# Top-32 attention and a SoLU layer on one core: steps of two chunks from each of two head pairs, with the weight check at the end

## The chip, the core and the metric

The kernel runs on one core of one Trainium2 chip. The core has a tensor engine (PE), a vector engine (DVE), a scalar engine (ACT), a general engine (POOL) and DMA queues that SyncE (SP) issues. Each engine works through its own instructions in order; across engines they wait for each other by semaphores. The metric is the time of one execution in device microseconds, smaller is better: a median over runs, beside one further execution that was profiled.

## The reference

```python
scores = scale * np.matmul(q, k.transpose(0, 1, 3, 2))          # B=8, H=8, S=576, D=64
kth = np.partition(scores, -32, axis=-1)[..., -32:-31]
scores = np.where(scores >= kth, scores, -1e9)
attn = softmax(scores)                                           # only the 32 largest of a row
x = (attn @ v).transpose(0, 2, 1, 3).reshape(4608, 512)
h = x @ w_in                                                     # 512 -> 1024
solu = h * softmax(h)
ln = (solu - mean(solu)) / sqrt(var(solu) + 1e-6) * g_ln
out = ln @ w_out                                                 # 1024 -> 512
```

The weights arrive as 64-bit numbers, everything is computed in 32 bits.

## The kernel before

The work is in `fast_path`. A general path behind it runs only if a flag (`bad`) is set at the end; it isn't reached here.

**A step** is one pair of heads of one batch (32 steps). Its 576 queries are four chunks of 128 and a tail of 64; with two heads that gives eight tiles of 128 queries x 576 keys, and a ninth in which the tails of both heads share the partitions. Per tile, the rank search and the softmax go through these instructions:

- PE forms scores (L816), ACT brings them to memory as `X` (L825).
- Counting. DVE counts the entries over a first threshold (`count0`, L833, tile `junkv`); two small operations form a second threshold (L841, L843). ACT counts against it (`count1`, a Sign with a sum, L849, tile `junka`). When all nine tiles are counted, `third` (L858, L862, L866 on DVE) forms the third threshold, and ACT counts again and leaves the signs (`count2`, L879, tile `sg`).
- Nearest. `side` (L888) picks a direction for three tiles at a time; `nearest` writes `w` on DVE (L900) and at once takes its eight largest (MAX8, L905). `kth` (five small DVE operations, L926 to L934) makes the exact 32nd largest value of all nine tiles.
- Softmax. ACT takes exponentials `E` (L913); DVE zeroes what lies under the 32nd and sums the rest (`keep`, L942); `inverse` (L950, L953) and POOL's `norm` (L957) divide.
- Product. PE transposes `E` (`tp_p` L971, `tp_pt` L1004), ACT copies to `PT` (L983 to L1012), PE multiplies with v (`om`, L1023), ACT copies to the token tiles `xTm` and `xTt` (L1034, L1037).

Ahead of a step its q, k and v are loaded and transposed, and PE and DVE estimate mean and spread of every row's scores (`y_ps` L737, `yq` L755, `ss` L766).

**A token tile** is 128 tokens of the second part; there are 36. PE `mm1` (`h_ps`, L1045), ACT `hexp` (L1056), DVE `solu` (L1061, L1064, L1068), ACT `square` (L1074), POOL `ln` (L1080 to L1085), PE transposes (`tp_ln`, L1092), ACT copies (L1098), PE `mm2` (`o_ps`, L1103), ACT copies to `osb` (L1110) and SP stores. A token tile needs all four head pairs of its queries, so the four tiles of batch b are placed beside steps 4(b+1) to 4(b+1)+3. The tails of two batches make one more tile. Those of the last batch come after the last step.

**Weights**: 16 pieces of 128x512. `w_bits` (three DVE operations, L579, L583, L587), `w_low` (ACT, L595), `w_mul`, `w_add` and `w_gain` (POOL) make 32-bit numbers; `w_check` (three ACT operations, L601, L604, L605) tests their exponents beside that.

**The order** is a table of places: every function has a number for a step, the step's index times 39 is added, and everything is sorted by that sum. The sorted order is the order in which PE, ACT, DVE and POOL get their instructions. DMA issues are not held to it. At the very end DVE counts in how many places the estimates and the weights lay in their bounds (`hit`, L1282), PE adds over partitions (`tp_ok`, L1287), and DVE sets `bad` (L1290), which the engines read and branch on.

Of the kernel before, what the change touches and what calls it, by code (L numbers as in the profile page):

```python
# [15 lines left out]
P = 128  # L16
# [427 lines left out]
def fast_path(  # L444
# [21 lines left out]

    nc = tc.nc
# [11 lines left out]
    SP = S // 2  # L479
# [69 lines left out]
    if not w_wide:  # L549
        nc.gpsimd.memset(w_ok, 512.0)  # L550
# [76 lines left out]
    st = [dict() for _ in pairs]  # L627
# [6 lines left out]
    def load_qk(i):  # L634
        b, hp = pairs[i]
        hh = slice(2 * hp, 2 * hp + 2)
        d = st[i]

        d["q"] = p1.tile([P, NT, D], F32, tag="qm", name="qm")
        d["k"] = p1.tile([P, 2 * NM, D], F32, tag="km", name="km")  # L640
        for nm, src in (("q", q), ("k", k)):
            nc.sync.dma_start(
                out=d[nm][:, 0 : 2 * NM, :].rearrange("p (t h) d -> p t h d", h=2),
                in_=src[b, hh, 0:SM, :].rearrange("h (p t) d -> p t h d", t=NM),
            )
# [26 lines left out]
    def pre_of(i):

        return once(st[i], "pre", lambda: ps_o.tile([P, 512], F32, tag="o", name="pre"))

    def prep_t(i):

        d = st[i]
        pre = pre_of(i)
        for n, nm in enumerate("qk"):  # L680
            nc.tensor.transpose(
                pre[:, n * ST : (n + 1) * ST], d[nm + "t"].rearrange("p h d -> p (h d)"),
# [3 lines left out]
    def prep_tc(i):  # L686
# [650 lines left out]
```

## Time and profile before

| | us |
|---|---|
| median of 3 runs (lowest to highest) | 1352.69 (1352.49 to 1354.34) |
| the profiled execution, its own time | 1354.09 |
| its span in the trace | 1352.3 |
| outside the span | 1.8 |
| PE, DVE, ACT, POOL busy, share of the span | 91%, 87%, 87%, 36% |
| chain of waits that ended last, by engine | DVE 52%, PE 27%, ACT 12% |

Busy time is an average over three different stretches. The page's strips cut the span into 40 slices of 33.8 us and give the busy share of each in tenths. In the first seven, when there are no token tiles or few, PE stands between 4 and 8 and its granted clock, at 9 in the first two, is at 6 or 7 tenths in the next four. From the ninth to the 36th PE stands at 9 with a clock at 9 (9 is 90% or more), and DVE and ACT at 8 or 9. In the last three PE works nearly alone: DVE stands at 0 or 1 and ACT at 2.

### The profile page before, as it was taken

How to read it: one execution, taken by the hardware profiler on the slowest of the kernel's cores; microseconds unless marked ns; L12 is line 12 of the kernel's file. 1: busy time of each engine (PE TensorE's matmuls, PEld its weight loads, DVE VectorE, ACT ScalarE, POOL GpSimd, SP SyncE). 2: the span in 40 equal slices, each digit the busy share in tenths (PEclk: the TensorE clock that was granted, in tenths of full speed). 3: DMA queues.
4: the chain of work that ended last, by engine and by line, in shares of the span. 5: the costliest groups of instructions: out<-in, count | busy, mean ns of one | idle time of the engine just before them, and what ended most of it. 6: DMA issues, size and time to landing. Idle time of an engine off the chain costs nothing.

```text
span 1352.3 us, 20269 instructions
## 1 busy us (share of the span) xinstructions
PE 1231.0 (91%) x6243; PEld 672.3 (50%) x6243; DVE 1183.2 (87%) x2766; ACT 1174.3 (87%) x2702; POOL 486.7 (36%) x584
## 2 busy tenths in 40 slices
PE   6476668999999999999999999999999999998997
PEld 3243434555555545555555545555555555554443
DVE  5799999999999989999999989899999989899010
ACT  6999899999999989899999989899999989896222
POOL 3245435443333323333333323333333333234110
PEclk9976679899999999999999999999999999999999
DMA  5112121011111111111111111111111111000001
GB/s 142 50 41 59 45 58 50 20 34 28 36 36 36 28 30 33 35 35 36 30 34 36 36 28 27 44 35 29 34 31 32 36 28 36 26 17 9 16 8 34
DMA packets 102404, 48.59 MB, mean 36 GB/s; under 512 B 87432, under 2 KB 95632, under 8 KB 102288
## 3 DMA queue, kind: packets, MB, share of 16 engines
q1 hardware_dynamic: 102288, 47.21, 13.0%
q8 instruction: 52, 0.85, 0.3%
q14 instruction: 64, 0.52, 0.1%
HBM read 37.75 MB, written 9.44 MB: 35 GB/s over the span
## 4 chain that ended last, share of the span: by engine, by line
DVE 52%; PE 27%; ACT 12%; issue 6%; DVEq 0%; ACTq 0%
DVE w L900 11%; DVE w L905 10%; DVE E L942 10%; PE o_ps L1103 8%; PE h_ps L1045 8%; DVE junkv L833 8%; ACT junka L849 4%; PE om L1023 3%; PE s_ps L816 3%; DVE solu L1064 2%; PE tp_p L971 2%; ACT sg L879 2%; DVE al L888 1%; ACT PT L983 1%; ACT X L825 1%
## 5 line engine op out<-in xcount | busy, mean ns | idle before, releaser
L957 POOL TENSOR_SCALAR E<-E,rden 128x576 f32<-128x576 f32 x256 | 239.3, 945 | 602.9 <-DVE step L858 496.6
L816 PE MATMUL s_ps<-qkT 64*128 64x288 f32 (+1 forms) x1280 | 259.1, 467 | 22.5 <-ACT X L825 11.6
L1103 PE MATMUL o_ps<-w_out,lnT 128*128 128x512 f32 x576 | 258.0, 593 | 0.0
L1045 PE MATMUL h_ps<-w_in,xTm 128*128 128x512 f32 x512 | 234.8, 603 | 0.0
L905 DVE MAX8 w<-w 128x8 f32<-128x576 f32 x288 | 219.2, 761 | 9.9
L900 DVE SCALAR_TENSOR_TENSOR w<-X,al,sg 128x576 f32<-128x576 f32 x256 | 220.9, 863 | 1.1
L942 DVE SCALAR_TENSOR_TENSOR E<-X,kth,E 128x576 f32<-128x576 f32 x256 | 212.2, 875 | 4.1 <-ACT junka L849 0.9
L879 ACT ACTIVATE sg<-X,t 128x576 bf16<-128x576 f32 x256 | 199.2, 787 | 15.5 <-DVE t L866 15.5
L849 ACT ACTIVATE junka<-X,t 128x576 bf16<-128x576 f32 x256 | 199.2, 801 | 2.1 <-DVE t L843 0.6
L816 PEld LDWEIGHTS s_ps<-qkT 64*128 64x128 f32 (+1 forms) x1280 | 143.1, 192 | 106.6 <-ACT X L825 38.4
L833 DVE TENSOR_SCALAR_CACHE_REDUCE junkv<-X,t 128x576 bf16<-128x576 f32 x256 | 192.0, 803 | 2.5 <-ACT X L825 2.5
L825 ACT ACTIVATE X<-s_ps 128x576 f32<-128x576 f32 x256 | 160.0, 660 | 34.5 <-PE s_ps L816 33.1
L971 PE MATMUL tp_p<-ident,E 128*128 128x128 f32 x1024 | 159.9, 293 | 13.2 <-POOL E L957 5.6
L1103 PEld LDWEIGHTS o_ps<-w_out,lnT 128*128 128x128 f32 x576 | 106.9, 190 | 120.9 <-issue 118.2
L913 ACT ACTIVATE E<-X 128x1152 f32<-128x1152 f32 x128 | 153.6, 1250 | 0.1
L983 ACT COPY PT<-tp_p 128x512 f32<-128x512 f32 x256 | 143.3, 606 | 7.8 <-PE tp_p L971 7.7
L971 PEld LDWEIGHTS tp_p<-ident,E 128*128 128x128 f32 x1024 | 117.0, 147 | 64.2 <-issue 20.2
L1045 PEld LDWEIGHTS h_ps<-w_in,xTm 128*128 128x128 f32 x512 | 92.7, 190 | 107.5 <-issue 106.0
L1023 PE MATMUL om<-PT,vm 128*64 128x288 f32 x1024 | 140.9, 418 | 0.0
L1023 PEld LDWEIGHTS om<-PT,vm 128*64 128x64 f32 x1024 | 68.9, 139 | 59.4 <-issue 20.6
L1056 ACT ACTIVATE e_sb<-h_ps 128x1024 f32<-128x1024 f32 x36 | 38.2, 1062 | 41.3 <-PE h_ps L1045 41.3
L1061 DVE RECIPROCAL rs<-sum_all 128x1 f32<-128x1 f32 x36 | 5.6, 156 | 64.7 <-ACT e_sb L1056 64.4
(132 smaller groups left out, 1706.4 us busy)
## 6 DMA issues: line engine op xcount, KB each, us to landing
qm<-in_q_dram SPq DMA_DIRECT2D x32, 256.0 KB, 3.4
km<-in_k_dram SPq DMA_DIRECT2D x32, 256.0 KB, 3.2
vm<-in_v_dram SPq DMA_DIRECT2D x32, 256.0 KB, 2.8
out_dram<-osb SPq DMA_DIRECT2D x32, 256.0 KB, 2.2
w_raw<-in_moe_w_in_dram SPq DMA_DIRECT2D x8, 512.0 KB, 3.8
w_raw<-in_moe_w_out_dram SPq DMA_DIRECT2D x8, 512.0 KB, 3.3
qt<-in_q_dram SPq DMA_DIRECT2D x32, 32.0 KB, 2.2
kt<-in_k_dram SPq DMA_DIRECT2D x32, 32.0 KB, 2.2
```

The lines of the kernel that those rows point to most:

```text
L816: nc.tensor.matmul(out=s[:, half, 0:SH], lhsT=qkT[hd, qs], rhs=qkT[hd, k0 : k0 + SH], start=True, stop=True,)
L833: nc.vector.tensor_scalar(out=junk, in0=x_of(i, j), scalar1=d["t0"][:, j : j + 1], scalar2=None, op0=ALU.is_ge, op1=ALU.add, accum_out=col ...
L849: nc.scalar.activation(out=junk, in_=x_of(i, j), func=AF.Sign, scale=-1.0, bias=d["t1"][:, j : j + 1], accum_out=columns(i, "n1")[:, j : j ...
L879: nc.scalar.activation(out=d["sg", j], in_=x_of(i, j), func=AF.Sign, scale=-(1.0 + 2.0**-23), bias=d["t2"][:, j : j + 1], accum_out=column ...
L900: nc.vector.scalar_tensor_tensor(out=w, in0=x_of(i, j), scalar=d["al"][:, j : j + 1], in1=d.pop(("sg", j)), op0=ALU.subtract, op1=ALU.mult,)
L905: nc.vector.max(w8[:, j, :], w)
L942: nc.vector.scalar_tensor_tensor(out=e, in0=x_of(i, j), scalar=d["kth"][:, j : j + 1], in1=e, op0=ALU.is_ge, op1=ALU.mult, accum_out=den_a ...
L957: nc.gpsimd.tensor_scalar(out=e, in0=e, scalar1=st[i]["rden"][:, j : j + 1], scalar2=1.0, op0=ALU.mult, op1=ALU.mult,)
L971: nc.tensor.transpose(tp[:, c, :], e[:, c * P : (c + 1) * P], ident)
L1023: nc.tensor.matmul(out=o[h * D : (h + 1) * D, 0:SP], lhsT=vm[:, h, c, :] if c < NM else vt[hd, :], rhs=pt[:, h * NM + c, :] if c < NM else ...
L1045: nc.tensor.matmul(out=h[:, half, :], lhsT=x[:, c, :], rhs=w_in[:, c, half * 512 : (half + 1) * 512], start=(c == 0), stop=(c == NP - 1),)
L1103: nc.tensor.matmul(out=o, lhsT=d["lnT"][:, c, :], rhs=w_out[:, c, :], start=(c == 0), stop=(c == NF - 1),)
```

## The change

- **Steps.** A step is now two chunks of one head pair and two chunks of another, of the same half of the batch, and the tail of one pair. Four steps still make a batch, and tiles, instructions on PE and their sizes stay as they were, except that the two attention products of a step are 320 and 256 columns wide and not 288 each. The work on k (`load_k`, `prep_k`, `moments`) is a list of its own, for each pair once. Both steps of a half need the keys of all four pairs. After two steps the first two token tiles of a batch are ready: they are placed beside step 4b+2+t, not 4(b+1)+t. After the last step three token tiles are left (two and the tails), not five.
- **Counts.** Of the nine `count1` of a step two (the second head of the fourth chunk, and the tails) go to DVE (L875). They count in another unit than ACT's, so `third` does its first two operations once for seven tiles and once for two.
- **MAX8 apart.** `nearest` is split in `nearest` (L953) and `best` (MAX8, L960), each with a place of its own.
- **Weight check.** `w_check` with its three ACT operations is gone from the start. Near the end all 16 pieces are loaded again into `X` buffers (`w_again`), DVE shifts out exponent bits (`w_exp`, L615), and one ACT operation each (L622) sums over them.
- **Buffers and copies.** `junkv`, `junka` and `osb` have one buffer, not two; k, v and the moments have four. One `copy_pt` instead of two, two instructions in `copy_last` instead of three, one copy of tails in `copy_v` instead of two per step.
- **Places.** All numbers of the table are new. q is loaded by four DMAs and not by one.

```diff
-    NPAIR = len(pairs)
+    steps = []
+    for b in range(B):
+        for half in range(2):
+            for n in range(NP // 2):
+                two = (2 * n + half, 2 * n + 1 - half)
+                chunks = [(hp, 2 * half + t) for hp in two for t in range(2)]
+                steps.append((b, chunks, two[0]))
+    NSTEP = len(steps)
...
+    def w_again(n):
+        raw = w_raw["again", n] = p8.tile([P, 512], mybir.dt.uint64, tag="X", name="w_again")
+        nc.sync.dma_start(out=raw, in_=w_chunks[n][1])
+
+    def w_exp(n):
+        w_tmp["exp", n] = p2.tile([P, 512], U32, tag="w", name="w_exp")
+        nc.vector.tensor_scalar(
+            out=w_tmp["exp", n], in0=words(("again", n), 1), scalar1=27, scalar2=15,
+            op0=ALU.logical_shift_right, op1=ALU.bitwise_and,
+        )
+
     def w_check(n):
-        f = low_of(n)[:, 1, :]
+        junk = p1.tile([P, S], BF16, tag="junka", name="junka")
         nc.scalar.activation(
-            out=f, in_=words(n, 1).bitcast(I32), func=AF.Square, scale=2.0**-27
-        )
-        nc.scalar.activation(out=f, in_=f, func=AF.Square, bias=m65)
-        nc.scalar.activation(
-            out=f, in_=f, func=AF.Sign, scale=-1.0, bias=p251, accum_out=w_ok[:, n : n + 1]
+            out=junk[:, 0:512], in_=w_tmp["exp", n].bitcast(I32), func=AF.Square, bias=m75,
+            accum_out=w_ok[:, n : n + 1],
         )
...
     def count1(i, j):
-        d = st[i]
-        junk = p2.tile([P, S], BF16, tag="junka", name="junka")
+        if j >= NT - N1:
+            count_v(i, j, "t1", "n1")
+            return
+        d = st[i]
+        junk = p1.tile([P, S], BF16, tag="junka", name="junka")
...
+        groups = ((slice(0, NT - N1), -513.0, -0.25), (slice(NT - N1, NT), -31.5, 0.5))
+        for js, less, _ in groups:
+            nc.vector.scalar_tensor_tensor(
+                out=w[:, js], in0=d["n1"][:, js], scalar=less, in1=d["tb"][:, js],
+                op0=ALU.add, op1=ALU.mult,
+            )
+        for js, _, part in groups:
+            nc.vector.scalar_tensor_tensor(
+                out=t2[:, js], in0=w[:, js], scalar=part, in1=d["t1"][:, js],
+                op0=ALU.mult, op1=ALU.add,
+            )
...
-        w = p2.tile([P, S], F32, tag="w", name="w")
+        w = d["w", j] = p2.tile([P, S], F32, tag="w", name="w")
...
+    def best(i, j):
         w8 = columns(i, "w8", NT * 8).rearrange("p (t e) -> p t e", e=8)
-        nc.vector.max(w8[:, j, :], w)
+        nc.vector.max(w8[:, j, :], st[i].pop(("w", j)))
...
-        (nearest, range(9), [41.97, 43.52, 51.69, 33.2, 29.56, 35.41, 57.15, 56.61, 53.25]),
+        (nearest, range(9), [41.07, 47.51, 39.3, 32.69, 29.76, 32.16, 57.74, 55.76, 51.21]),
+        (best, range(9), [46.43, 52.3, 45.06, 36.45, 31.16, 33.82, 59.19, 58.14, 52.97]),
...
-        n = NP * (b + 1)
-        last = b == B - 1
+        n = NP * b + 2
         for t in range(NM):
...
-            if last:
-                all_times(n * STEP + 15.0 * t, last_times, d)
+            if n + t >= NSTEP:
+                all_times(NSTEP * STEP + 15.0 * (n + t - NSTEP), last_times, d)
             else:
-                all_times((n + t) * STEP, token_times, d)
+                all_times((n + t) * STEP, token_times if b else first_times[t], d)
```

How the rows of the table now fall is seen in the instructions' order. First DVE within a step, at the nearest values: before, `w` (L900) and the MAX8 that reads it (L905) stand together, with the small operations of `inverse` (L950, L953) and `side` (L888) between the couples.

```order
L888 SCALAR_TENSOR_TENSOR al<-n_5442,tt 128x3
L900 SCALAR_TENSOR_TENSOR w<-X,al,sg 128x576
L905 MAX w_5568<-w 128x8
L950 TENSOR_SCALAR rden<-den_all 128x3
L953 RECIPROCAL rden<-rden 128x3
L900 SCALAR_TENSOR_TENSOR w<-X,al,sg 128x576
L905 MAX w_5568<-w 128x8
L888 SCALAR_TENSOR_TENSOR al<-n_5442,tt 128x3
L900 SCALAR_TENSOR_TENSOR w<-X,al,sg 128x576
L905 MAX w_5568<-w 128x8
L785 TENSOR_TENSOR t_5621<-mean,zs 128x9
L787 SCALAR_TENSOR_TENSOR ta<-tb,t_5621 128x9
```

After, on the same engine in a step: `w` is L953, MAX L960, and L875 are counts (into `c` against the first threshold, into `n` against the second); L941 is `side`, L886 and L888 are the two operations of the second threshold, L981 begins `kth`.

```order
L953 SCALAR_TENSOR_TENSOR w<-X,al,sg 128x576
L875 TENSOR_SCALAR junkv,c_4074<-Xt,t_4063 128x576
L941 SCALAR_TENSOR_TENSOR al<-n_3914,tt 128x3
L886 TENSOR_TENSOR u<-c_4074,tb 128x9
L888 TENSOR_TENSOR t_4194<-u,ta 128x9
L953 SCALAR_TENSOR_TENSOR w<-Xt,al,sg 128x576
L960 MAX w_4002<-w 128x8 x2
L953 SCALAR_TENSOR_TENSOR w<-X,al,sg 128x576
L875 TENSOR_SCALAR junkv,n_4220<-X,t_4194 128x576
L953 SCALAR_TENSOR_TENSOR w<-X,al,sg 128x576
L960 MAX w_4002<-w 128x8 x2
L981 TENSOR_TENSOR hot<-ranks,far 128x72
```

Something else now stands between a `w` and its own MAX, and the operation on the first counts (L886) no longer follows the last count directly.

DVE again, from the end of `kth` (L934 before) to `third` (L858 to L866), with the `keep`s (L942) around it; before:

```order
L931 TENSOR_REDUCE zk_all<-hot 128x9
L933 TENSOR_TENSOR kth<-al,zk_all 128x9
L934 SCALAR_TENSOR_TENSOR kth<-kth 128x9
L942 SCALAR_TENSOR_TENSOR E,den_all<-X,kth,E 128x576 x4
L950 TENSOR_SCALAR rden<-den_all 128x3
L953 RECIPROCAL rden<-rden 128x3
L858 SCALAR_TENSOR_TENSOR step<-n_5323,tb 128x9
L862 SCALAR_TENSOR_TENSOR t_5419<-step,t_5286 128x9
L866 TENSOR_SCALAR t_5419<-t_5419 128x9
L942 SCALAR_TENSOR_TENSOR E,den_all<-X,kth,E 128x576 x3
```

After, `kth` ends with L989, the `keep`s are L997, `third` is L909 to L919, and L875 is a count:

```order
L988 TENSOR_TENSOR kth<-al,zk_all 128x9
L989 SCALAR_TENSOR_TENSOR kth<-kth 128x9
L875 TENSOR_SCALAR junkv,n_4220<-Xt,t_4194 128x576
L997 SCALAR_TENSOR_TENSOR E,den_all<-X,kth,E 128x576 x3
L909 SCALAR_TENSOR_TENSOR step<-n_4220,tb 128x7
L909 SCALAR_TENSOR_TENSOR step<-n_4220,tb 128x2
L914 SCALAR_TENSOR_TENSOR t_4305<-step,t_4194 128x7
L914 SCALAR_TENSOR_TENSOR t_4305<-step,t_4194 128x2
L919 TENSOR_SCALAR t_4305<-t_4305 128x9
L997 SCALAR_TENSOR_TENSOR E,den_all<-X,kth,E 128x576 x3
```

A count stands between `kth` and the first `keep`, and `third` has five instructions in place of three.

PE after the last attention product, before (from the fourth row; ahead of it are 4 of `h_ps` and 8 of `o_ps`; a matmul of 512 columns counts once here, and twice in the trace):

```order
L1045 MATMUL h_ps<-w_in,xTm 128x512 x16
L1092 MATMUL tp_ln<-ident,solu 128x128 x8
L1045 MATMUL h_ps<-w_in,xTm 128x512 x4
L1103 MATMUL o_ps<-w_out,lnT 128x512 x4
L1045 MATMUL h_ps<-w_in,xTm 128x512 x4
L1092 MATMUL tp_ln<-ident,solu 128x128 x8
L1045 MATMUL h_ps<-w_in,xTm 128x512 x4
L1103 MATMUL o_ps<-w_out,lnT 128x512 x8
L1045 MATMUL h_ps<-w_in,xTt 128x512 x4
L1092 MATMUL tp_ln<-ident,solu 128x128 x8
L1045 MATMUL h_ps<-w_in,xTt 128x512 x4
L1103 MATMUL o_ps<-w_out,lnT 128x512 x8
```

After, from the last attention product to the end of the work:

```order
L1157 MATMUL o_ps<-w_out,lnT 128x512 x4
L1099 MATMUL h_ps<-w_in,xTm 128x512 x8
L1157 MATMUL o_ps<-w_out,lnT 128x512 x4
L1099 MATMUL h_ps<-w_in,xTm 128x512 x8
L1146 MATMUL tp_ln<-ident,solu 128x128 x8
L1099 MATMUL h_ps<-w_in,xTt 128x512 x8
L1157 MATMUL o_ps<-w_out,lnT 128x512 x4
L1146 MATMUL tp_ln<-ident,solu 128x128 x8
L1157 MATMUL o_ps<-w_out,lnT 128x512 x8
L1146 MATMUL tp_ln<-ident,solu 128x128 x8
L1157 MATMUL o_ps<-w_out,lnT 128x512 x12
```

Of `h_ps` 24 stand behind the last attention product and not 40, of `o_ps` 32 and not 48, of `tp_ln` 24 and not 40. On ACT one `w_check` (L622) stands behind the last copy to `osb`, and on DVE two `w_exp` stand ahead of the last `keep`s. Ahead of the last `keep` stand 33 `solu`, and 31 before.

## Rows read from the trace of the kernel before

**Rows 1.** Profile page, part 1: engine busy us (share of the span) xinstructions
```profile
PE 1231.0 (91%) x6243; PEld 672.3 (50%) x6243; DVE 1183.2 (87%) x2766; ACT 1174.3 (87%) x2702; POOL 486.7 (36%) x584
```

**Rows 2.** Busy time by stretch: span, then PE, PEld, DVE, ACT, POOL, (instructions); PEclk, DMA, GB/s
```profile
307.40:454.60 147.20, 141.80 (x760) 77.45 (x760) 142.74 (x336) 138.50 (x324) 53.55 (x64) 1.00 0.13 33
454.60:607.70 153.10, 150.68 (x785) 81.92 (x783) 143.37 (x340) 140.61 (x328) 55.53 (x67) 1.00 0.13 33
1248.60:1264.70 16.10, 14.46 (x92) 8.24 (x90) 1.21 (x10) 7.64 (x18) 6.24 (x9) 1.00 0.05 18
1264.70:1345.00 80.30, 80.29 (x220) 37.62 (x218) 8.31 (x26) 20.11 (x38) 9.65 (x15) 1.00 0.04 17
```

**Rows 3.** Waits of DVE from 270 to 1200 us: total, times, longest
```profile
DVE step L858 <- ACT junka L849: 8.2, 3, 2.9
DVE yq L755 <- PE y_ps L737: 7.3, 3, 2.4
```

**Rows 4.** Timeline of DVE in one step: start us, duration us, line, operation, tiles
```profile
783.05 0.81 DVE L833 TENSOR_SCALAR_CACHE_REDUCE junkv<-X,t 128x576 bf16<-128x576 f32 x1
783.78 0.16 DVE L888 SCALAR_TENSOR_TENSOR al<-n,tt 128x3 f32<-128x3 f32 x1
783.86 0.81 DVE L833 TENSOR_SCALAR_CACHE_REDUCE junkv<-Xt,t 128x576 bf16<-128x576 f32 x1
784.70 0.17 DVE L841 TENSOR_TENSOR u<-c,tb 128x9 f32<-128x9 f32 x1
...
789.54 0.80 DVE L900 SCALAR_TENSOR_TENSOR w<-X,al,sg 128x576 f32<-128x576 f32 x1
790.38 0.76 DVE L905 MAX8 w<-w 128x8 f32<-128x576 f32 x1
...
792.04 0.17 DVE L934 SCALAR_TENSOR_TENSOR kth<-kth 128x9 f32<-128x9 f32 x1
792.31 0.82 DVE L942 SCALAR_TENSOR_TENSOR E<-X,kth,E 128x576 f32<-128x576 f32 x1
793.06 0.81 DVE L942 SCALAR_TENSOR_TENSOR E<-X,kth,E 128x576 f32<-128x576 f32 x1
793.80 0.81 DVE L942 SCALAR_TENSOR_TENSOR E<-X,kth,E 128x576 f32<-128x576 f32 x1
```

**Rows 5.** Timeline of DVE and then of POOL, 797 to 800 us
```profile
798.09 1.28 DVE L942 SCALAR_TENSOR_TENSOR E<-X,kth,E 128x576 f32<-128x576 f32 x1
...
797.46 2.52 POOL L957 TENSOR_SCALAR E<-E,rden 128x576 f32<-128x576 f32 x2
```

**Rows 6.** Groups by line and form: busy us, mean ns of one
```profile
L833 DVE TENSOR_SCALAR_CACHE_REDUCE junkv<-X,t 128x576 bf16<-128x576 f32 x256 | 192.0, 803 | 2.5 <-ACT X L825 2.5
L587 DVE TENSOR_SCALAR w_tmp<-w_tmp 128x512 uint32<-128x512 uint32 x16 | 8.4, 526 | 0.5
```

**Rows 7.** Timeline of PE, after the last attention product
```profile
1288.82 1.04 PE L1092 MATMUL tp_ln<-ident,solu 128*128 128x128 f32 x8
1289.70 3.60 PE L1045 MATMUL h_ps<-w_in,xTm 128*128 128x512 f32 x8
1293.13 3.60 PE L1103 MATMUL o_ps<-w_out,lnT 128*128 128x512 f32 x8
```

**Rows 8.** Timeline near the end: DVE, PE, ACT
```profile
1245.76 1.28 DVE L1064 SCALAR_TENSOR_TENSOR solu<-h_ps,rs,e_sb 128x1024 f32<-128x1024 f32 x1
1247.89 0.81 DVE L942 SCALAR_TENSOR_TENSOR Et<-Xt,kth,Et 128x576 f32<-128x576 f32 x1
...
1344.80 0.19 PE L1287 MATMUL tp_ok<-ok,ones 128*1 128x6 f32 x2
...
1344.95 0.58 ACT L1110 COPY osb<-o_ps 128x512 f32<-128x512 f32 x1 [6.28 <-PE o_ps L1103]
```

**Rows 9.** The start: DVE's first row of step 0; DMA issues, us to landing
```profile
12.91 0.69 DVE L755 TENSOR_TENSOR yq<-y_ps,qm 128x512 f32<-128x512 f32 x1 [1.97 <-PE y_ps L737]
...
km<-in_k_dram SPq DMA_DIRECT2D x32, 256.0 KB, 3.2
```

More of the change, by code (lines that the diff above doesn't have):

```diff
@@ L623, in w_gain @@
         )
-    st = [dict() for _ in pairs]
+    ks = [dict() for _ in pairs]
+    st = [dict() for _ in steps]
     xs = {}
@@ L672, in pre_of, with mom_of, prep_t @@
[L672 to L680, printed above, removed]
+    def mom_of(n):
+        return once(ks[n], "mom", lambda: p4.tile([P, D + 1], F32, tag="mom", name="mom"))
+    def pre_of(n):
+        return once(ks[n], "pre", lambda: ps_o.tile([P, 512], F32, tag="o", name="pre"))
+    def prep_t(n):
+        d = ks[n]
+        pre = pre_of(n)
+        for m, nm in enumerate("qk"):
@@ L721, in moments, with moments_c, load_q, keys_of @@
                 )
-    def moments_c(i):
+    def moments_c(n):
+        nc.scalar.copy(out=mom_of(n)[:, 0:D], in_=ks[n]["tm"])
+    def load_q(i):
+        b, chunks, x = steps[i]
         d = st[i]
-        nc.scalar.copy(out=mom_of(i)[:, 0:D], in_=d["tm"])
+        d["q"] = p1.tile([P, NT, D], F32, tag="qm", name="qm")
+        for c, (hp, t) in enumerate(chunks):
+            nc.sync.dma_start(
+                out=d["q"][:, 2 * c : 2 * c + 2, :],
+                in_=q[b, 2 * hp : 2 * hp + 2, 0:SM, :].rearrange("h (p t) d -> p t h d", t=NM)[
+                    :, t, :, :
+                ],
+            )
+        for h in range(2):
+            nc.sync.dma_start(
+                out=d["q"][h * ST : (h + 1) * ST, 2 * NM, :], in_=q[b, 2 * x + h, SM:S, :]
+            )
+    def keys_of(i, c):
+        b, chunks, x = steps[i]
+        return ks[NP * b + (x if c == NM else chunks[c][0])]
+    def queries_of(i, c):
+        return keys_of(i, c)["kT"][:, 0:ST] if c == NM else st[i]["qT"][:, c * P : (c + 1) * P]
+    def prep_q(i):
+        st[i]["tp_q"] = transposed(st[i]["q"])
+    def prep_qc(i):
+        st[i]["qT"] = p2.tile([P, SM], F32, tag="qT", name="qT")
+        nc.scalar.copy(out=st[i]["qT"], in_=st[i]["tp_q"])
     def spread(i):
@@ L1183, in fast_path @@
[L1183 to L1184 removed]
+        (mm1, range(2), [62.78, 58.57]),
+        (hexp, [()], [65.23]),
+        (solu, [()], [66.07]),
+        (square, [()], [69.08]),
+        (ln, [()], [77.72]),
+        (transpose_ln, range(2), [104.86, 122.87]),
+        (copy_ln, range(2), [106.51, 124.77]),
+        (mm2, range(2), [123.9, 126.46]),
+        (store, [()], [129.25]),
     ]
     last_times = [
[L1188 to L1189 removed]
@@ L1197, in fast_path @@
+        (mm2, range(2), [103.52, 117.24]),
+        (store, [()], [177.72]),
     ]
```

405 lines of the change are left out of this document (219 added, 186 removed).

## The prediction

> **What bounds the kernel now.** I read the page's busy times first. PE is at 91% of the span, DVE and ACT at 87% [rows 1]: from shares as near as these no engine can be called the limit, so I went to the view by stretch. Four steps in the steady part show two kinds of stretch. In 307.4:454.6 DVE is busy 142.74 of 147.2 us, and the rest is gaps between operations that need each other's results: DVE sets the pace, 36.8 us a step. In 454.6:607.7, where a tails tile comes in, PE is busy 150.68 of 153.1 and DVE 143.37: PE sets it, 38.3 us a step [rows 2]. The waits of DVE say the same thing: in 930 us it waits 8.2 us for ACT's second count (three times) and 7.3 us for PE's `y_ps` (three times) [rows 3]. So up to the last `keep` the time is DVE's work plus 15.5 us of waits, with ACT and PE close behind.
>
> Then comes a different stretch. The last `keep` starts at 1247.89 and the last attention product ends about 1264.7; until 1345 PE is busy 80.29 of 80.3 us and DVE 8.31 [rows 2, 8]. Here PE is the only limit. An instruction moved from this stretch to before 1248 takes time off PE alone and gives it to stretches in which PE has a little room.
>
> **The change, term by term**, against the span of 1352.3 us.
>
> *Counts.* Two of nine second counts go from ACT to DVE. Back to back a count costs DVE 0.73 us (783.05 to 783.78) [rows 4]; two are +1.46 a step. `third` gets two more small operations; independent ones start 0.08 apart (783.78 to 783.86) [rows 4], and standing between dependent ones they save some of that again: +0.1. ACT loses two counts; it isn't the limit here, so its saving shows only in waits, below.
>
> *MAX8 apart from its `w`.* A `w` that is followed by its own MAX8 holds it for 0.84 us (789.54 to 790.38), while a two-input operation of the same size followed by one that doesn't need it holds it for 0.745 (two gaps from 792.31 to 793.80) [rows 4]. In the new order nearly every MAX8 has another operation between; nine times 0.095 is −0.86 a step. The bounds: nothing, and a saving of 0.84 − 0.73 = 0.11 each, −1.0 a step.
>
> *Two more couples parted.* The first `keep` now waits for `kth` behind a count: 0.27 (792.04 to 792.31) becomes 0.08, −0.19. The operation behind the last first count started 0.84 after it (783.86 to 784.70) and now needs 0.73 with `side` between [rows 4]: −0.11.
>
> A step of DVE is therefore 1.46 + 0.10 − 0.86 − 0.19 − 0.11 = +0.40 us, and 32 steps are **+12.8**. Collisions are taken as unchanged: while POOL divides, DVE's `keep` can take 1.28 in place of 0.81 [rows 5]. The added counts add none: the 256 first counts average 0.803 [rows 6], their undisturbed duration.
>
> *The start.* The first `yq` is at 12.91 and already waited for PE [rows 9]. Now the first step needs keys of two pairs, and the second load of k goes into the same buffer, so it starts when PE has read the first. A load lands in 3.2 us [rows 9]; with a little of PE's transposing that is **+3.5**. It can be 0 if other early waits cover it, and twice 3.2 and more, 7, if the queue is in the way.
>
> *Token tiles ahead of the last `keep`.* 33 `solu` stand there, not 31. From a `solu` to what follows its small operation is 1.40 us (1245.76 to 1247.89, less one `keep` at 0.73) [rows 8]; with the reciprocal ahead 1.6, so two are **+3.2**. Two `w_exp` stand there too, priced like the 128x512 operation at L587, 0.43 and on average 0.526 with its collisions [rows 6]: **+0.9**. The weights' own operations on DVE are the same number, only earlier.
>
> *Waits.* ACT gets 1.5 us less to do per step, and token tiles stand one or two to a step as before. Whether the 15.5 us of DVE's waits go depends on places I can't time. The ends are 0 and 15.5, and nothing is nearer to one than to the other; I take half, **−7.7**. What is late next where a wait goes is DVE itself. The single buffers (`junka`, `junkv`, `osb`) are each reused by the engine that wrote them, in order, or after a store of a few us; I cost them at nothing, because a next count on the same engine starts after the earlier one anyway. Without that cover ACT would pay some 0.1 us a count, 0.7 a step, on an engine that has 8 us of room in 147 [rows 2].
>
> *The last stretch.* One half of `h_ps` or `o_ps` takes PE 3.43 us (1289.70 to 1293.13), a tile's transposes 0.88 (1288.82 to 1289.70) [rows 7]. Behind the last product stood 40 + 48 matmuls in groups of four, 22 halves, and 40 transposes, 5 tiles: 22 × 3.43 + 5 × 0.88 = 79.9, which is the stretch as measured. Now there are 24 + 32, 14 halves, and 3 tiles: 50.7. So **−29.2**. PE stays fed: between a tile's `h_ps` and its transposes there are three halves of other work or more, 10 us, and the way through ACT, DVE and POOL takes about 7. The 16.1 us between last `keep` and last product [rows 2] I leave as they are.
>
> *The end.* `tp_ok` follows the last matmul directly at 1344.80 while ACT's last copy runs from 1344.95 for 0.58 [rows 8]. Now it waits for that copy, then for a last `w_check` of the size of one operation like the copy with its sum, some 0.8, and a count: **+2.0**, between 1 and 3. The other reloads and checks lie beside PE's last stretch, where ACT is busy 20.11 of 80.3 [rows 2].
>
> The sum: 12.8 + 3.5 + 3.2 + 0.9 − 7.7 − 29.2 + 2.0 = −14.5; span 1337.8, with the 1.8 us outside it 1339.6. The profiled execution was 1.4 above the median, so the forecast on the median's scale is **1338 us**.
>
> **Rivals.**
>
> *The steps get shorter too (1315).* All of the waits go, 7.8 us more than I took. And one `keep` in each step stops colliding with POOL, 0.47 us each [rows 5], 15 us over 32 steps. For it: the divisions are placed later after their `keep`s than before. Against it: POOL does as many, and whether a DVE operation lies beside them is chance. 1338 − 7.8 − 15 = 1315.
>
> *The gain is eaten (1353).* The same mechanism the other way: one more `keep` or `w` a step collides, +15. As much would come from PE, which had 2.4 us of room in a tails stretch of four steps [rows 2] and has the same work in a stretch that DVE should now leave sooner. 1353, within a fifth of a per cent of before or just under.
>
> *Slower: parting the couples saves nothing (1366).* If DVE starts no large operation before the one ahead of it has emptied its pipe, whatever it needs, then a `w` with a count behind it costs what it cost with its MAX8. Then nine times 0.095 in 32 steps, 27.4, isn't saved, and DVE has paid for 64 counts with nothing: 1338 + 28 = 1366. It decides once more than half of the 27.4 fails to come (14.5 is the whole gain). For it: the trace of before has not one `w` with anything but its MAX8 behind it, so 0.745 is borrowed from `keep`. Against it: two `keep`s start 0.74 apart though each lasts 0.81 [rows 4], so the second starts before the first has ended, and two counts do likewise.
> The Trainium skill has this rule: "VectorE: DVE Perf Modes", section "The DRAIN you can't avoid", says that the next operation does not start until the pipe is empty and that leaving out semaphores doesn't avoid it. By that the answer would be 1366. The trace agrees only in part, with 0.74 against 0.81; the same page's section on two Vector instructions with no wait between them says that one that isn't held starts earlier, which is what the rows look like.
>
> **How the numbers follow.** The forecast gets 0.55, the shorter steps 0.18, the eaten gain 0.13, the slower case 0.14. Around 1338 the open terms (start 0 to 7, waits 0 to 15.5, end 1 to 3, the parted couples 0.02 either way on 288) make 1325 to 1350. The range that should hold 8 in 10 reaches from the shorter steps' 1315 to above the eaten gain, 1357; the slower case and the far half of the first rival lie outside. What differs by under 0.2% can't be told from no change here. Faster: 0.55 + 0.18 and 0.05 of the eaten gain, 0.78. Same: 0.05. Slower: 0.14 and 0.03 of the eaten gain, 0.17.
>
> **What would show it.** In the profile after: a `w` followed by something other than its MAX8 has that start about 0.74 later (0.84 would be the slower case). DVE's busy time up by about 64 × 0.81 = 52 us for the counts, less what the overlap hides. Steps of 36 to 38 us without the difference between stretches with and without a tails tile; DVE's waits for the second count gone. From the end of the last product to `tp_ok` 51 to 53 us. The first `yq` at 16 to 17. I am wrong if the last `keep` ends later than about 1275, or if PE waits for normed tiles in the last stretch.

## The result and the profile after

| | before | after |
|---|---|---|
| median of 4 runs (us) | 1352.99 | 1300.02 (1299.94 to 1300.61) |
| ratio, 95% interval | | 0.961 (0.959 to 0.963) |
| span of the profiled execution | 1352.3 | 1298.1 |
| last operation of `third` in the first step | 37.96 | 43.44 |
| the same in the sixth step | 234.67 | 237.65 |
| the same in the last step | 1214.03 | 1186.15 |
| last attention product ends | 1264.7 | 1236.4 |
| `tp_ok` starts | 1344.80 | 1289.57 |

The kernel became 53 us faster; I had forecast 15, and 1315 as the lower end. The span is 54.2 shorter, and the table says where: the first six steps cost 3.0 more, the 26 steps behind them take 30.9 less, and from the last product to `tp_ok` it is 53.1 us and not 80.1, 27.0 less. The rest is small: 0.4 less between the two, and 1.0 more behind `tp_ok`.

The page's busy times answer to [rows 1]. DVE has 64 counts more and is busy 28 us less, at 89% of the span. (PE is busy 36 us less with the same matmuls; why, I did not follow up.)

```profile
PE 1194.8 (92%) x6243; PEld 658.0 (51%) x6243; DVE 1154.8 (89%) x2974; ACT 1118.8 (86%) x2446; POOL 479.6 (37%) x583
```

By stretch, as in [rows 2] (span, PE, PEld, DVE, ACT, POOL): a period of eight steps, in it four steps without a tails tile and the two with one; last, from the last product to `tp_ok`.

```profile
531.12:823.69 292.57, 289.38 (x1561) 159.55 (x1561) 275.98 (x724) 273.23 (x600) 107.16 (x131) 1.00 0.13 34
566.11:706.16 140.05, 137.85 (x760) 76.39 (x759) 136.59 (x361) 134.53 (x297) 53.54 (x64) 1.00 0.14 35
706.16:788.40 82.24, 81.72 (x434) 44.91 (x433) 71.20 (x185) 71.61 (x162) 27.02 (x35) 1.00 0.16 40
1236.40:1289.60 53.20, 51.30 (x140) 23.65 (x138) 12.93 (x37) 23.69 (x53) 5.83 (x9) 1.00 0.19 65
```

In the steps without a tails tile DVE is still the limit, at 35.0 us a step where it was 36.8; PE follows at 137.85 of 140.05. In the two with one PE is busy 81.72 of 82.24: it is the limit, and these two became 2.1 us longer together. Eight steps take 292.57 us (from 531.12 to 823.69 by `third`'s last operation), where they took 300.88. The step of DVE can be read between two executions of that operation (start, duration):

```profile
601.21 0.17 DVE L919 TENSOR_SCALAR t<-t 128x9 uint32<-128x9 uint32 x1
...
636.19 0.17 DVE L919 TENSOR_SCALAR t<-t 128x9 uint32<-128x9 uint32 x1
```

34.98 us, with next to no waiting between. DVE's waits did not vanish. By their longest kinds they grew from 15.5 us (270 to 1200, [rows 3]) to 27.1 (270 to 1150):

```profile
DVE step L909 <- ACT junka L897: 12.4, 7, 3.1
DVE E L997 <- ACT E L968: 9.6, 3, 3.3
DVE yq L798 <- PE y_ps L780: 5.1, 3, 1.7
```

What shrank is DVE's work itself. The table adds up the times from one start to the next over four steps without a tails tile (16th to 19th), by function, in us a step (`nearest` with `best`, its MAX8); its sums are 36.78 and 35.01. It was worked out from the timelines, of which single rows follow.

| | before | after | forecast of the difference |
|---|---|---|---|
| counts (9, then 11) | 6.70 | 8.21 | +1.35 (with the operation behind) |
| `nearest` and MAX8 | 14.11 | 12.65 | −0.86 |
| `keep` | 7.30 | 6.63 | 0 |
| `first` (two small operations) | 1.09 | 0.38 | 0 |
| `side` (three small operations) | 0.97 | 0.60 | 0 |
| `third` | 0.81 | 0.55 | +0.10 |
| `kth` | 1.26 | 1.06 | −0.19 |
| `inverse` | 1.08 | 1.31 | 0 |
| waits and everything else | 3.46 | 3.62 | 0 |

The couples: a `w` (first row) now holds DVE for 0.73 us, where it was 0.84 [rows 4].

```profile
624.27 0.81 DVE L953 SCALAR_TENSOR_TENSOR w<-X,al,sg 128x576 f32<-128x576 f32 x1
625.00 0.80 DVE L875 TENSOR_SCALAR_CACHE_REDUCE junkv<-Xt,t 128x576 bf16<-128x576 f32 x1
...
613.90 0.17 DVE L828 TENSOR_TENSOR t<-mean,zs 128x9 f32<-128x9 f32 x1
614.20 0.17 DVE L830 SCALAR_TENSOR_TENSOR ta<-tb,t 128x9 f32<-128x9 f32 x1
614.29 0.81 DVE L875 TENSOR_SCALAR_CACHE_REDUCE junkv<-X,t 128x576 bf16<-128x576 f32 x1
```

The two small operations at 613.90 and 614.20 (`first`) take 0.17 us each. Before, the same ones were 0.493 and 0.610 on average. The averages of four groups of DVE in the changed kernel, to be held against [rows 6] for the first (mean ns behind the busy time):

```profile
L875 DVE TENSOR_SCALAR_CACHE_REDUCE junkv<-X,t 128x576 bf16<-128x576 f32 x288 | 230.7, 801 | 11.9 <-ACT X L867 7.3
L997 DVE SCALAR_TENSOR_TENSOR E<-X,kth,E 128x576 f32<-128x576 f32 x256 | 200.0, 818 | 9.7 <-ACT E L968 9.6
L830 DVE SCALAR_TENSOR_TENSOR ta<-tb,t 128x9 f32<-128x9 f32 x32 | 7.2, 225 | 4.0
L919 DVE TENSOR_SCALAR t<-t 128x9 uint32<-128x9 uint32 x32 | 5.5, 173 | 1.1
```

Counts are what they were. A `keep` averages 0.818 us, 0.875 before; the second small operation of `first` 0.225, 0.610 before; `third`'s last 0.173, 0.584 before. POOL's divisions have not become fewer. They lie elsewhere: three from 604.08 beside a `solu`, which reads PSUM, and four from 614.26 beside counts.

```profile
604.08 2.58 POOL L1012 TENSOR_SCALAR E<-E,rden 128x576 f32<-128x576 f32 x3 [1.91 <-DVE rden L1008]
614.26 2.91 POOL L1012 TENSOR_SCALAR E<-E,rden 128x576 f32<-128x576 f32 x4
```

One operation of `inverse` still starts in the first of these stretches, and one of `side` in the single division right behind the second; they take 0.49 and 0.54.

The last stretch, PE, for [rows 7, 8]: from the last product to the last matmul PE has one gap of 0.17 us, and `tp_ok` waits 1.73 us for the last weight check.

```profile
1235.86 0.65 PE L1075 MATMUL om<-PT,vt 64*64 64x256 f32 x4
...
1280.70 7.13 PE L1157 MATMUL o_ps<-w_out,lnT 128*128 128x512 f32 x16 [0.17 <-ACT osb L1164]
1289.57 0.19 PE L1402 MATMUL tp_ok<-ok,ones 128*1 128x6 f32 x2 [1.73 <-DVE hit L1397]
```

### The profile page after: what moved, and what is told of

Same layout as the page of the kernel before. It is cut to its first block, busy times and chain, and to the rows that moved or that the text cites. A ratio compares the mean times of both kernels' runs of the same rounds, so it can differ in the third digit from the quotient of the medians.

```text
span 1298.1 us, 20306 instructions
## 1 busy us (share of the span) xinstructions
PE 1194.8 (92%) x6243; PEld 658.0 (51%) x6243; DVE 1154.8 (89%) x2974; ACT 1118.8 (86%) x2446; POOL 479.6 (37%) x583
## 4 chain that ended last, share of the span: by engine, by line
PE 59%; ACT 18%; DVE 15%; issue 3%; POOL 3%; DMA 1%; SPq 0%; DVEq 0%; POOLq 0%; ACTq 0%
PE o_ps L1157 15%; PE s_ps L858 12%; PE h_ps L1099 12%; PE tp_p L1026 7%; PE om L1075 7%; DVE junkv L875 4%; ACT junka L897 4%; DVE E L997 3%; ACT sg L932 3%; ACT PT L1038 2%; PE tp_ln L1146 2%; ACT E L968 2%; DVE w L953 2%; DVE w L960 2%; ACT X L867 2%
## 5 line engine op out<-in xcount | busy, mean ns | idle before, releaser
L875 DVE TENSOR_SCALAR_CACHE_REDUCE junkv<-X,t 128x576 bf16<-128x576 f32 x288 | 230.7, 801 | 11.9 <-ACT X L867 7.3
L1012 POOL TENSOR_SCALAR E<-E,rden 128x576 f32<-128x576 f32 x256 | 204.7, 813 | 87.0 <-DVE rden L1008 76.5
L925 POOL TENSOR_SCALAR tt<-t 128x9 f32<-128x9 f32 x32 | 21.8, 680 | 573.3 <-DVE t L919 573.3
L953 DVE SCALAR_TENSOR_TENSOR w<-X,al,sg 128x576 f32<-128x576 f32 x256 | 210.6, 824 | 0.1
L960 DVE MAX8 w<-w 128x8 f32<-128x576 f32 x288 | 210.5, 749 | 0.0
L997 DVE SCALAR_TENSOR_TENSOR E<-X,kth,E 128x576 f32<-128x576 f32 x256 | 200.0, 818 | 9.7 <-ACT E L968 9.6
L858 PE MATMUL s_ps<-kT,qT 64*128 64x288 f32 x1024 | 195.7, 458 | 5.5 <-ACT X L867 4.5
L897 ACT ACTIVATE junka<-X,t 128x576 bf16<-128x576 f32 x224 | 174.3, 778 | 19.4 <-DVE t L888 15.6
L1026 PEld LDWEIGHTS tp_p<-ident,E 128*128 128x128 f32 x1024 | 116.0, 144 | 92.9 <-issue 37.5
L1075 PE MATMUL om<-PT,vm 128*64 128x256 f32 (+1 forms) x1024 | 140.0, 416 | 0.0
L858 PEld LDWEIGHTS s_ps<-kT,qT 64*128 64x128 f32 x1024 | 116.2, 199 | 46.7 <-ACT X L867 18.1
L818 POOL TENSOR_TENSOR zs<-zs,phalf 128x9 f32<-128x9 f32 x32 | 70.2, 2194 | 2.7
```

What stands on the lines that cost most here:

```text
L858: nc.tensor.matmul(out=s[:, half, 0:SH], lhsT=queries_of(i, t)[hd, :], rhs=kT[hd, k0 : k0 + SH], start=True, stop=True,)
L875: nc.vector.tensor_scalar(out=junk, in0=x_of(i, j), scalar1=st[i][t][:, j : j + 1], scalar2=None, op0=ALU.is_ge, op1=ALU.add, accum_out=co ...
L897: nc.scalar.activation(out=junk, in_=x_of(i, j), func=AF.Sign, scale=-1.0, bias=d["t1"][:, j : j + 1], accum_out=columns(i, "n1")[:, j : j ...
L953: nc.vector.scalar_tensor_tensor(out=w, in0=x_of(i, j), scalar=d["al"][:, j : j + 1], in1=d.pop(("sg", j)), op0=ALU.subtract, op1=ALU.mult,)
L960: nc.vector.max(w8[:, j, :], st[i].pop(("w", j)))
L997: nc.vector.scalar_tensor_tensor(out=e, in0=x_of(i, j), scalar=d["kth"][:, j : j + 1], in1=e, op0=ALU.is_ge, op1=ALU.mult, accum_out=den_a ...
```

## The experiments

Theories: **A**, what an operation of DVE costs depends on whether POOL is in a division when it starts, and the new order moved them apart; **B**, these operations have their durations of their own. **C**, a `w` not followed by its MAX8 is 0.1 cheaper; **D**, it isn't. **E** and **F** on the counts are in their run's expectation. Each ratio is to the kernel before; the changed kernel's own is 0.961. Work is DVE's time from start to start without its waits, in the four steps of the table.

**1. The divisions moved in the kernel before.**

```diff
-        (inverse, range(3), [60.22, 65.15, 70.68]),
+        (inverse, range(3), [63.0, 65.15, 70.68]),
-        (norm, range(9), [61.06, 60.35, 61.47, ...
+        (norm, range(9), [63.06, 63.01, 63.47, ...
-        (spread_v, [()], [-13.48]),
+        (spread_v, [()], [-14.3]),
     ... transpose_p, its first two: 63.34, 62.61 -> 63.53, 63.52
```

> The kernel before, with one thing moved: the first inverse of a step stands behind three more keeps and the estimate of the next step ahead of the last two, so that POOL's first three divisions lie beside operations that read PSUM. Theory A (what a DVE operation costs depends on what POOL does beside it): the last operation of third falls from 0.55 to 0.1 from start to start and the keep that took 1.22 takes 0.74, so a step without a tails tile goes from 36.80 to 35.9 us; the total falls by 0.9 times about 20 steps, to 1332 to 1338. Rival B (the steps of the changed kernel are shorter for the couples parted alone, and these two operations are long for reasons of their own): 36.8 stays and 1352.

Measured: 1391 us, 1.028 (1.026 to 1.030). The total went the other way. Its timeline (DVE) shows `third`'s last operation at 0.17 and the operations beside the three moved divisions undisturbed, but a wait in front of `yq`:

```profile
695.20 0.17 DVE L866 TENSOR_SCALAR t<-t 128x9 uint32<-128x9 uint32 x1
698.45 1.28 DVE L1064 SCALAR_TENSOR_TENSOR solu<-h_ps,rs,e_sb 128x1024 f32<-128x1024 f32 x1
700.64 0.69 DVE L755 TENSOR_TENSOR yq<-y_ps,qm 128x512 f32<-128x512 f32 x1 [0.71 <-PE y_ps L737]
```

DVE's own work, without waits, fell from 36.78 to 35.30 us a step: the costs are A's. The waits from 270 to 1150 us took it back and more:

```profile
DVE yq L755 <- PE y_ps L737: 25.2, 22, 4.2
DVE rs L1061 <- ACT e_sb L1056: 17.4, 22, 3.7
DVE step L858 <- ACT junka L849: 16.1, 21, 3.1
```

In this step PE forms the estimate `y_ps` 5.1 us behind `third`'s last operation and transposes the first divided tile at 10.3; before, it was 1.6 and 2.0. So a division's place seems to have two prices, what starts beside it and who waits for it; my expectation had only the first. How much of the waits is the divisions' and how much comes of `yq`, which this edit also placed sooner, no run separates.

**2. The divisions moved back in the changed kernel.**

```diff
-        (inverse, range(3), [62.57, ...
+        (inverse, range(3), [60.6, ...
-        (keep, range(9), [60.36, 61.34, 60.51, ...
+        (keep, range(9), [60.36, 60.45, 60.51, ...
-        (norm, range(9), [66.71, 64.69, ...
+        (norm, range(9), [66.71, 61.0, ...
```

> The changed kernel, with the first inverse of a step directly behind its first three keeps and POOL's first division ahead of its other work, as before. Theory A: the collisions of third's last operation and of a keep are back, 0.9 us a step; steps without a tails tile go from 34.98 to 35.9 us, those with one stay at 40 to 42 as PE sets them; total 1310 to 1318. Rival B: 34.98 and 1300 stay.

Measured: 1316 us, 0.972 (0.969 to 0.974); steps without a tails tile 35.76. As A has it. DVE first, then POOL:

```profile
646.35 0.79 DVE L997 SCALAR_TENSOR_TENSOR E<-X,kth,E 128x576 f32<-128x576 f32 x1
647.06 0.71 DVE L909 SCALAR_TENSOR_TENSOR step<-n,tb 128x7 f32<-128x7 f32 x2
648.82 0.82 DVE L997 SCALAR_TENSOR_TENSOR E<-X,kth,E 128x576 f32<-128x576 f32 x1
649.56 1.29 DVE L997 SCALAR_TENSOR_TENSOR E<-X,kth,E 128x576 f32<-128x576 f32 x1
```

```profile
646.62 1.14 POOL L1012 TENSOR_SCALAR E<-E,rden 128x576 f32<-128x576 f32 x1 [18.52 <-DVE rden L1008]
648.94 2.53 POOL L1012 TENSOR_SCALAR E<-E,rden 128x576 f32<-128x576 f32 x2
```

The first two operations of `third`, at 647.06, start inside POOL's division of 646.62 and take 0.71 together, where they took 0.23. The `keep` at 648.82 starts ahead of a division and takes 0.82; the one at 649.56 starts inside one and takes 1.29.

**3 and 4. No division at all**, in both kernels (output not normalised).

```diff
     def norm(i, j):
-        e = p_of(i, j)
-        nc.gpsimd.tensor_scalar(...)
+        return
```

> The kernel before without POOL's division of the probabilities (L957 left out, 288 operations). Theory A: DVE's collisions with POOL's divisions end, 2.7 us a step by the start-to-start times of the operations that were long beside one (last of third 0.45, a keep 0.48, a w 0.48, side 0.43 and 0.2, the two of first 0.3 and 0.4); DVE's own work falls from 36.8 to 34.1 us a step, the steps to PE's 35 or DVE's 34.1, total 1310 to 1325. Rival B: DVE's durations stay, 36.8 and 1350.

> The changed kernel without POOL's division. Theory A: little is left to gain, 0.7 us a step of DVE's work (inverse 0.4, one side 0.3), and PE takes over at 34.7: steps without a tails tile 34.5 to 34.8 us, total 1292 to 1298. Rival B, that the divisions cost DVE as much here as before: 33 us of DVE's work a step.

Measured: 1322 us, 0.977 (0.976 to 0.979), and 1288 us, 0.951 (0.950 to 0.953), the second under the 1292 to 1298 expected; 5 us of its gain lie in the first six steps, which I had not counted. DVE's work without waits fell from 36.78 to 34.79 us a step in the kernel before, and from 34.89 to 34.45 in the changed one. The collisions with divisions cost 2.0 us a step before and 0.4 after. The groups in the kernel before without divisions:

```profile
L942 DVE SCALAR_TENSOR_TENSOR E<-X,kth,E 128x576 f32<-128x576 f32 x256 | 196.5, 815 | 3.3
L787 DVE SCALAR_TENSOR_TENSOR ta<-tb,t 128x9 f32<-128x9 f32 x32 | 6.5, 204 | 3.6
L866 DVE TENSOR_SCALAR t<-t 128x9 uint32<-128x9 uint32 x32 | 5.6, 173 | 1.1
```

They are at the changed kernel's means with the divisions in (0.818, 0.225, 0.173). The forecast of 2.7 was too high, since one operation of `inverse` met POOL's `ln` instead (`inverse` takes 1.72 us a step, 1.08 with the divisions).

**5. Only the couples parted, in the kernel before.**

```diff
...
-        nc.vector.max(w8[:, j, :], w)
+    def best(i, j): nc.vector.max(w8[:, j, :], st[i].pop(("w", j)))
...
+        (best, range(9), [43.525, 43.57, 53.26, 35.42, 33.21, 38.3, 57.3, 57.16, 56.62]),
```

> The kernel before with its MAX8 as a function of its own, placed behind the next operation of DVE; nothing else is changed. Theory C (a w that isn't followed by its own MAX8 is 0.1 cheaper): nine w take 7.0 us and not 8.0 from start to start, steps without a tails tile go from 36.8 to 35.8 us, total 1328 to 1336. Rival D (an operation starts when the pipe is empty, whatever it needs): w stays at 0.84, 36.8 and 1352.

Measured: 1331 us, 0.983 (0.982 to 0.985); 35.65 us a step. C holds, D is out: a `w` with another `w` behind holds DVE for 0.73 us. This edit alone takes some 23 us off the kernel before.

```profile
694.27 0.81 DVE L900 SCALAR_TENSOR_TENSOR w<-X,al,sg 128x576 f32<-128x576 f32 x1
695.00 0.81 DVE L900 SCALAR_TENSOR_TENSOR w<-Xt,al,sg 128x576 f32<-128x576 f32 x1
695.73 0.75 DVE L907 MAX8 w<-w 128x8 f32<-128x576 f32 x1
```

Of the 1.1 us a step 0.9 is `nearest` with MAX8; 0.5 came from `first` and `side`, which left POOL's divisions, and 0.5 went into waits.

**6. The couples back together, in the changed kernel.**

```diff
-        (best, range(9), [46.43, 52.3, 45.06, ...
+        (best, range(9), [41.0701, 47.5101, 39.3001, ...   # each directly behind its nearest
```

> The changed kernel with each MAX8 directly behind its w again. Theory C: nine w cost 7.6 us from start to start and not 6.5, steps without a tails tile 36.0 us and not 34.98, total 1312 to 1320, unless collisions shift as well. Rival D: 34.98 and 1300.

Measured: 1352 us, 0.998 (0.997 to 0.999): all of the gain is gone. The step is 37.5 us, 2.5 more and not the 1.0 of C. DVE:

```profile
672.46 0.79 DVE L953 SCALAR_TENSOR_TENSOR w<-X,al,sg 128x576 f32<-128x576 f32 x1
673.28 0.76 DVE L960 MAX8 w<-w 128x8 f32<-128x576 f32 x1
673.96 0.62 DVE L828 TENSOR_TENSOR t<-mean,zs 128x9 f32<-128x9 f32 x1
674.70 0.61 DVE L830 SCALAR_TENSOR_TENSOR ta<-tb,t 128x9 f32<-128x9 f32 x1
...
683.46 0.80 DVE L875 TENSOR_SCALAR_CACHE_REDUCE junkv<-X,t 128x576 bf16<-128x576 f32 x1
684.39 0.81 DVE L875 TENSOR_SCALAR_CACHE_REDUCE junkv<-X,t 128x576 bf16<-128x576 f32 x1
```

The `w` is back at 0.82 (672.46 to 673.28): +1.09 a step. The two of `first` are back at 0.62 and 0.61, since POOL's four divisions now begin ahead of them, at 673.83: +0.91. And counts that follow each other directly start 0.93 us apart (0.95 the next), not 0.73: with one buffer `junkv` a count starts only behind the end of the one before, which lasts 0.80. In the changed kernel one such pair stands in a step (614.29 to 615.23, with MAX8 or `w` between the others), here four: +0.62. So of what a MAX8's place is worth, less than half is its own couple.

**7. The two counts back on ACT, in the changed kernel.**

```diff
-    N1 = 2
+    N1 = 0
...
-        groups = ((slice(0, NT - N1), -513.0, -0.25), (slice(NT - N1, NT), -31.5, 0.5))
+        groups = ((slice(0, NT), -513.0, -0.25),)
```

> The changed kernel with all nine second counts on ACT again. Theory E (the two counts had to leave ACT for the shorter step): DVE would need 33.4 us a step, but ACT, busy 33 to 34 of 35 us, gets 1.5 more; steps without a tails tile 35.3 to 35.8 us with DVE waiting for ACT's last count at third, total 1304 to 1316. Rival F (ACT has room, so the counts cost DVE 47 us for nothing): steps fall to PE's 34.7, those with a tails tile stay, total 1294 to 1300.

Measured: 1394 us, 1.028 (1.025 to 1.031); 38.0 us a step. E's direction, with more than its size. DVE's work falls to 33.9 a step, and then it waits at `third` for ACT's last count:

```profile
643.30 0.08 DVE L997 DVE_READ_ACCUMULATOR E<-X,kth,E 128x1 f32 x1
648.36 0.17 DVE L909 SCALAR_TENSOR_TENSOR step<-n,tb 128x9 f32<-128x9 f32 x1 [4.98 <-ACT junka L897]
```

In 292 us it waits 39.7 there. ACT's `junka` start 0.90 us apart here, as in the changed kernel, and 0.76 in the kernel before, which had two buffers for them; no run changes that buffer alone. That the places are those of seven counts makes this an upper bound of what two counts cost on ACT; other places for nine were not tried.

**8 and 9. The weight check left out**, after and before (the tile of its sums is filled with a constant).

```diff
-        (w_check, w_wide, range(NW), [
+        (w_check, False, range(NW), [        # after: w_again and w_exp as well
```

> The changed kernel without its weight check (no second load, no w_exp, no w_check; the tile that it fills is set to a constant). My term of the end: tp_ok comes directly behind the last matmul again, 1.7 us sooner, and two w_exp leave the way to the last keep; total 1297 to 1299. If the reloads at the end cost more than that (DMA or X buffers in the way of the last steps), 1293 or less.

> The kernel before without its weight check (three ACT operations for each of 16 pieces left out; the tile that they fill is set to a constant). If the first steps are DVE's, as its 97% busy there says, ACT's 34 us are off the path: 1350 to 1354. Rival: the check held the buffers in which weights are made, or ACT itself was the limit of the first eight steps, and moving it is worth 5 us or more: 1340 to 1347.

Measured: 1299 us, 0.958 (0.957 to 0.960), 1 to 4 us less than with the check; and 1351 us, 0.997 (0.996 to 0.998), some 4 us less. Moving the check is worth between nothing and 3 us: not a part of the 53 that can be told apart.

**10. The last two token tiles late**, in the changed kernel without its check.

```diff
-        n = NP * b + 2
+        n = NP * b + 2 if b < B - 1 else NSTEP
-            all_times(NSTEP * STEP + 30.0, last_times, d)
+            all_times(NSTEP * STEP + 60.0, last_times, d)
-        (store, [()], [177.72]),
+        (store, [()], [128.12]),
```

> The changed kernel without its weight check and with the last batch's first two token tiles behind the last step, so that five tiles are left there, as before. To be read against the changed kernel without its check alone. My term of the last stretch: 20 halves and 5 tiles of transposes behind the last product and not 14 and 3, 73.0 us and not 50.7, less 3.3 for two solu fewer in the last steps: 18 to 20 us slower. Rival: the steps that lose the tiles were PE's and give as much back: within 5 us.

Measured: 1314 us, 0.971 (0.969 to 0.972) against 0.958 without the edit, 15 us slower. From the last product to `tp_ok` 73.2 us (50.8 without):

```profile
1228.58 0.65 PE L1075 MATMUL om<-PT,vt 64*64 64x256 f32 x4
...
1302.41 0.19 PE L1402 MATMUL tp_ok<-ok,ones 128*1 128x6 f32 x2
```

22.4 longer, as reckoned, and the last `keep` is 6.6 sooner, twice what I took for it, so 15 and not 18 to 20. The last stretch's term holds.

**11. Two buffers for DVE's counts, and the last check earlier.**

```diff
-        junk = p1.tile([P, S], BF16, tag="junkv", name="junkv")
+        junk = p2.tile([P, S], BF16, tag="junkv", name="junkv")
     w_exp 11: 1452.18 -> 1445.18; w_check 11: 1493.58 -> 1449.58
```

> The changed kernel with two buffers for DVE's counts again (adjacent counts start 0.94 apart with one buffer, 0.73 with two) and the last w_check and w_exp ahead of the last copy to osb. DVE saves 0.2 us a step where it sets the pace and the end 1.7 us: steps 34.8, total 1294 to 1297. If PE has taken over in every step, only the end: 1298.

Measured: 1292 us (5 runs, 1288.6 to 1293.5), 0.954 (0.953 to 0.956): faster than both kernels, and under the 1294 to 1297 expected. Adjacent counts start 0.73 apart again: counts fall by 0.2 us a step, and `side`, which left a division, by 0.3; most of the steps that DVE set are 34.4 to 34.9 us long. PE is now all but fully busy in both kinds of stretch, 138.89 of 140 and 81.48 of 82:

```profile
566.00:706.00 140.00, 138.89 (x753) 76.83 (x752) 136.46 (x367) 135.58 (x301) 54.61 (x65) 1.00 0.13 35
706.00:788.00 82.00, 81.48 (x442) 44.78 (x440) 69.32 (x182) 70.74 (x158) 25.87 (x35) 1.00 0.16 40
```

## Why the prediction was wrong

**The step that failed** is "Collisions are taken as unchanged". I had seen one, a `keep` at 1.28 for 0.81 [rows 5], and let at most one a step come or go. There were seven in a typical step of the kernel before: in `third`, `first` twice, `side` twice, a `keep`, a `w`; six with a division, and one `side` with POOL's `ln`. Two are left after. Those with divisions cost 2.0 us a step, 0.4 in the new order (3 and 4), and order alone brings or loses them (2 and 6). Their rows were in the trace of before: `first`'s second operation at 0.610 on average where an operation of its size takes 0.17 [rows 4]. Three of one step, DVE and then POOL:

```profile
759.26 0.64 DVE L866 TENSOR_SCALAR t<-t 128x9 uint32<-128x9 uint32 x1
767.44 0.36 DVE L888 SCALAR_TENSOR_TENSOR al<-n,tt 128x3 f32<-128x3 f32 x1
767.83 1.28 DVE L900 SCALAR_TENSOR_TENSOR w<-X,al,sg 128x576 f32<-128x576 f32 x1
...
759.13 0.74 POOL L957 TENSOR_SCALAR E<-E,rden 128x576 f32<-128x576 f32 x1 [20.25 <-DVE step L858]
766.60 1.19 POOL L1085 TENSOR_SCALAR solu<-solu,nmu,rstd 128x1024 f32<-128x1024 f32 x1
767.77 0.75 POOL L957 TENSOR_SCALAR E<-E,rden 128x576 f32<-128x576 f32 x1
```

What I overlooked in them is how long a collision lasts: until POOL's operation has ended. When the small one at 759.26 starts, 0.61 of a division is left, and it takes 0.64; at 767.44 0.35 of `ln` is left, and it takes 0.36; at 767.83 0.69 of a division is left, and the `w` takes 0.6 more than that, 1.28.

I priced the instructions that the diff changes and left the rest at what they took, though the table moved every one of them. My terms made a step 0.40 us longer and it became 1.77 shorter. The 2.2 between are the unforecast falls of `first` (0.71), `keep` (0.67), `nearest` with MAX8 (0.60), `side` (0.37) and `third` (0.36), less 0.5 that came on elsewhere. Not all of this is collisions: in `nearest` a part is the couples, below.

The Trainium skill, "GPSIMD Engine Reference", section "1. Specifications", says that POOL shares its SBUF interfaces with DVE and contends with instructions of two SBUF inputs or in a 2-port mode. The trace agrees for the large ones: a `keep` and a `w`, with two inputs from SBUF, took up to 1.29 beside a division, and counts, with one, 0.80 throughout. What mode the small ones with one input are in, as `third`'s last, no run here shows.

**What would then have bounded it** stood in [rows 2] as well, roughly: PE is busy 141.80 + 150.68 = 292.5 us in eight steps, and the eight steps after take 292.57. DVE alone would need eight times 35.0 and one more `solu`, 282. I named PE as close behind and did not add it up as a floor. That the two figures meet is luck, though: after, PE is busy 289.38 in its eight steps with the same matmuls, and in the steps without a tails tile DVE sets the pace; without the divisions (4) and with two buffers (11) eight steps take 291.2, less than the sum. My rival of shorter steps had the mechanism, at a chance of 0.18, with one collision a step for the five that went, and without the floor.

**The terms.** *Counts*: +1.35 forecast with the operation behind; +1.51, the rest being the one adjacent pair that the single `junkv` delays by 0.2. "I cost them at nothing" was wrong for the single buffers: 0.2 us a count that follows a count on DVE (6, 11); on ACT 0.14, if the buffer is the cause there (7). *MAX8 apart*: right in kind and about in size, 0.10 apiece for 0.095: without divisions (3, 4) the nine `w` and MAX8 take 13.66 us a step and 12.72. The rival with nothing saved is out (5). *`kth`*: −0.20 for −0.19. *The start*: the first `yq` at 18.44 for 16 to 17, behind a third set of weight bits whose load DVE awaited for 5.8 us; by the sixth step 3.0 us of it were left, for 3.5. *`solu` and `w_exp`*: ahead of the last `keep` as reckoned, but in steps that PE sets or that were shorter anyway; not seen apart. *Waits*: half of 15.5 us forecast to go; none did. DVE waits 27.1 us in 880, in and around the steps with a tails tile, where PE is the limit. *The last stretch*: −27.0 with the check's 1.7 in it, so −28.7, for −29.2. *The end*: +1.7 for +2.0. *Per step*: +0.40 was charged to all 32 steps, though by my own reading PE, not DVE, set those with a tails tile. *Buffers and copies*: what ACT's fewer copies are worth alone, no run shows.

Of the signs I named, the 0.74 behind a parted `w` and the 51 to 53 us of the last stretch came. DVE's busy time fell by 28 us and did not rise, the steps are 35 and 41 us and not alike, and the waits for the second count stayed.

## What to carry to other kernels

When a change reorders everything, first mark in the trace of before each operation that takes longer than its twin, and ask of each what lay beside it; those are what a new order can win or bring, and they can outweigh every instruction that the diff counts. Then add up each engine's busy time over a whole period: the largest sum is a rough floor (PE's came out 1% high here), and the forecast starts from the larger of the critical engine's work and that floor. A single output buffer that nobody reads still orders the instructions that write it; put something else between them, or give it a second.

## What was not expected of the hardware

- An operation of 128x3 or 128x9 on DVE that starts while POOL is in a division of 128x576 mostly lasts until the division has ended: 0.3 to 0.7 us for 0.15 to 0.17, by what is left of it. A two-input operation of 128x576 takes some 0.60 more than what is left, up to 1.29 for 0.81. Not all are held: counts and MAX8 never were, nor the reciprocals of `inverse` (0.18) or `solu`, which reads PSUM (1.28).
- One that started ahead of the division takes its normal time, and POOL's division is then the longer one: in experiment 2 the `keep` at 646.35 takes 0.79 and the division at 646.62 takes 1.14 for 0.74.
- Two counts that write the same buffer start 0.93 to 0.95 us apart on DVE (0.73 with two buffers). On ACT it is 0.90 with one buffer and 0.76 with two, read across two kernels.
